# Attention with beacon keys, then an ELU MLP: a new order of the opening's loads and of all steps, tiles 0 and 1 with one ScalarE pass per ELU, and all copies of turned q and k of batches 1 and 2 on VectorE

## The chip, the cores and the metric

One core of one Trainium2 chip runs the kernel. The metric is the device time of one execution in microseconds (us), median of the runs; lower is better. Engines are named as in the profile: PE (TensorE matmul), PEld (its weight loads), DVE (VectorE), ACT (ScalarE), POOL (GpSimd), SP (SyncE). PSUM, which PE writes, has eight banks here, shared out by name: two "ops", two "hps", and two pairs "S".

## The reference

Inputs are float32: q, k, v of 8 batches x 8 heads x 576 tokens x 64, sixteen beacon keys and values for each batch and head, w_in 512 x 2048, w_out 2048 x 512. The attention is causal over the tokens, and the beacons are seen by all; then an MLP with ELU runs over 4608 tokens.

```python
scores = scale * np.matmul(q, k_all.transpose(0, 1, 3, 2))   # k_all: beacons first
scores = np.where(causal, -1000000000.0, scores)
a = np.exp(scores - scores.max(-1, keepdims=True))
a /= a.sum(-1, keepdims=True) + 1e-09
attn = np.matmul(a, v_all)
x = attn.transpose(0, 2, 1, 3).reshape(B * S, H * D)
h = x @ w_in
g = np.where(h > 0.0, h, np.exp(np.minimum(h, 0.0)) - 1.0)
return g @ w_out
```

## The kernel before

**An order written out by hand.** The kernel defines small steps (Python functions) and a text of 1489 words that says in which order they are issued, as "F.0.1" for F(0, 1). No scheduler changes that order: each engine runs its own instructions strictly in the order of the list, and waits where one needs something of another engine. So a step that waits holds up everything behind it on its engine, and DMAs issued by POOL wait behind POOL's other work. A DMA of POOL also waits, in both kernels, for the landing of the one eight issues ahead of it.

**Attention of a batch b** (p is a pair of heads, 0 to 3):

- lq (L132, issue L136) loads q and k through POOL, tokens on partitions; batch 0 in two runs of tokens (0 to 255, 256 to 575) and two halves of the heads, batch 1 in two halves of the heads, batch 2 whole. lv (L141, issues L144 and L149) loads v in five blocks of keys and the beacons' v. Batches 3 to 7 come instead through a scratch copy (lk, L754, POOL) and a transposing DMA (lt, L761, SP); lp (L769, L770, POOL) sets the beacon columns.
- T (L254, matmuls L266) turns q and k of a pair on PE, into an "hps" bank for batch 0 and an "S" pair for batches 1 and 2. ck (L283) copies the result out of PSUM on ACT, cq (L287) on DVE (both are recorded at L279). cb (L275) adds the beacon columns.
- S (L308, matmuls L320) makes scores by groups of columns into an "S" pair; x (L329, exp at L335) takes the exponential on ACT; m (L340) multiplies the causal mask on DVE (the mask is made on POOL by tri, L238 and L240).
- L (L401) makes the row sums, n (L434, L437) their inverse on ACT by a logarithm and an exponential, W (L377) the product with v, M (L471, L481, L488) scales it on DVE into xT, the input of the MLP. For batch 0 there are two parts of the tokens, A and B. D (L393, DVE) adds up exponentials ahead of L from batch 3 on.

**The MLP** runs over ten tiles of tokens: 0 and 1 of 256, the others of 512. F(t, i) (L502, matmuls L511) makes one bank "hps" of h from w_in, with sixteen F for a tile of 512 and eight for one of 256. The ELU has two forms:

```python
# u, k: two passes over PSUM on ACT (e and u), one instruction on DVE
e:  eb = exp(h)                     # ACT, L521
u:  rb = relu(h)                    # ACT, L526
kk: half = min(eb - 1, rb)          # DVE, L536, from SBUF
# r, g: one pass on ACT (e), two instructions on DVE
r:  rb = min(eb, 1) - 1             # DVE, L543, from SBUF
g:  half = max(h, rb)               # DVE, L548, reads h in PSUM
```

In the first form u frees the bank of h (e has read it too), in the second g does. G (L557) multiplies by w_out for tiles 0 and 1, o and s write them out. From tile 2 on the second product goes by a seven-product scheme of half tiles: Z (L578) forms sums of the activations on DVE, Q (L621) multiplies into "ops" banks, J (L630, L637, L635) moves and adds the results and stores them. wt (L578) forms the sums of w_out that it needs, and H (L578) those of w_in for the last tiles 8 and 9 (P, L691; K, E, U, V), where the first product uses seven products as well. The first H (H.1) writes into the tile that the beacon keys arrived in, which also holds the rows of zeros that the filler matmuls read.

**Loads of the weights.** wi(c) (L157, issues L161) loads half of w_in's columns in eight DMAs of 128 KB (as stored), wo (L164) a quarter of w_out in one of 512 KB. An F of tile 0 or 1 with i under 4 needs all eight DMAs of the first half.

**Fillers.** warm and wm (L205, L213) are matmuls into a bank that nobody reads, to keep PE busy; wm(n) has n units of 128 columns.

In the list of before, the loads stand between the steps: batch 0's q and k in four parts, v block 2, half of batch 1, v blocks 0 and 1, the first half of w_in, v blocks 3 and 4, the other half of batch 1, the second half of w_in, w_out.

Of the kernel before, what the change touches and what calls it, by code (L numbers as in the profile page):

```python
# [17 lines left out]
def kernel(  # L18
# [81 lines left out]
    w_in16 = konst.tile([P, NCC, DF], FP16, name="w_in16")  # L100
# [12 lines left out]
    st, vt = {}, {}  # L113
# [39 lines left out]

# [3 lines left out]
    def load_wi(c):  # L157
        f_ = slice(DF // 2 * c, DF // 2 * (c + 1))
        for g in range(2):
            for i in range(4):  # L160
                nc.gpsimd.dma_start(  # L161
                    out=w_in16[32 * i:32 * (i + 1), 2 * g:2 * g + 2, f_], in_=wi_v[i, :, g, :, f_])
# [86 lines left out]
    @step  # L249
    def wi(c):  # L250
        load_wi(c)
# [532 lines left out]
    lq.0.0.0.4 warm.12 ident bt T.0.1.0 bk cb.0.0 wm.7 T.0.0.0 ck.0.1.0 cb.0.1 S.0.1.0  # L784
    lq.0.1.0.4 cq.0.0.0 wm.8 T.0.0.1 cb.0.2 x.0.1.0 S.0.0.0 x.0.0.0 cq.0.0.1 T.0.1.1 wm.8
    S.0.0.2 tri lq.0.0.4.8 T.0.2.0 ck.0.1.1 S.0.1.2 T.0.3.0 x.0.0.2 cq.0.3.0 cq.0.2.0 x.0.1.2
    S.0.1.1 x.0.1.1 wm.6 S.0.1.3 cb.0.3 wm.6 S.0.3.0 x.0.1.3 lq.0.1.4.8 m.0.0.2 m.0.0.0 lv.0.2
    x.0.3.0 T.0.2.1 cq.0.2.1 S.0.0.3 x.0.0.3 wm.8 S.0.2.0 T.0.3.1 x.0.2.0 S.0.2.3 x.0.2.3
    m.0.3.0 cb.1.1 wm.4 S.0.2.2 cq.0.3.1 wm.6 S.0.3.3 lq.1.0.0.4 x.0.2.2 x.0.3.3 m.0.2.0 wm.6
    S.0.0.1 x.0.0.1 m.0.1.0 L.0.A T.1.0.0 lv.0.0.1 n.0.A cq.1.0.0 m.0.0.3 T.1.1.0 W.0.A.0  # L790
    W.0.A.1 M.0.A.0 M.0.A.1 m.0.1.3 S.0.2.1 cb.1.2 ck.1.1.0 m.0.2.2 cb.1.0 S.1.5 m.0.2.3 x.0.2.1
    wi.0 x.1.5 S.1.3 x.1.3 S.0.3.1 x.0.3.1 S.0.3.2 x.0.3.2 F.0.1 e.0.1 S.1.1 r.0.1 g.0.1 S.1.4
    x.1.4 F.0.0 S.1.2 F.0.2 x.1.1 x.1.2 u.0.0 lv.0.3.4 lq.1.0.4.8 e.0.2 m.0.3.2 m.0.1.2 m.0.3.3
    L.0.B n.0.B e.0.0 wi.1 W.0.B.0 M.0.B.0 W.0.B.1 M.0.B.1 wo.0 r.0.2 T.1.2.0 F.1.1 ck.1.2.0
    g.0.2 T.1.3.0 e.1.1 u.1.1 S.1.6 x.1.6 F.0.4 F.1.7 e.0.4 k.0.0 cq.1.3.0 S.1.11 S.1.7 m.1.1.0
# [137 lines left out]
```

## Time and profile before

| | us |
|---|---|
| median of three runs (335.95 to 339.8) | 336.29 |
| span of the profiled execution, first to last instruction | 335.3 |
| PE busy (share of the span) | 324.6 (97%) |
| PEld busy | 206.8 (62%) |
| DVE busy | 280.0 (84%) |
| ACT busy | 282.5 (84%) |
| POOL busy | 87.9 (26%) |

The span is that of one profiled execution; its whole time is not listed, and the median of the runs is 1.0 above the span. Idle time of an engine costs something only where the engine is on the chain that ends last. A busy PE is not PE at its peak: matmuls are pipelined and their ends are modelled, and the row counts a matmul as busy until its modelled end. In the page's view by slices the span is cut in 40 slices of 8.4 us; a digit is the busy share in tenths:

```profile
PE   7979899999999999999999999999999999999995
DVE  3652988666899999997999889988999998998962
ACT  2998798899999999989898889897987677988930
POOL 8875749360049106500160060000000000000000
DMA  9999999999939997996099495000101021010212
```

### The profile page before, as it was taken

The page shows a single profiled execution, that of the slowest core. Times are in us where ns is not written, and L with a number is a line of the kernel's source. Part 1 is how long each engine was busy: PE and PEld are TensorE (multiplying, and loading weights), DVE is VectorE, ACT ScalarE, POOL GpSimd, SP SyncE. Part 2 cuts the span into 40 slices and gives each one's busy share as a digit, 9 for nine tenths or more (in the row PEclk, how much of TensorE's full clock was granted, in tenths as well). Part 3 has the DMA queues.
Part 4 walks back from the last instruction along what each step waited for, and adds up shares of the span by engine and source line. Part 5 has one row for each costly group of instructions (what it writes and reads, how often), then busy time and mean ns, then how long its engine had stood idle before and what let it go on. Part 6 is the DMA issues. An engine that isn't in the chain of part 4 may idle for free.

```text
span 335.3 us, 8722 instructions
## 1 busy us (share of the span) xinstructions
PE 324.6 (97%) x3561; PEld 206.8 (62%) x3561; DVE 280.0 (84%) x592; ACT 282.5 (84%) x460; POOL 87.9 (26%) x121
## 2 busy tenths in 40 slices
PE   7979899999999999999999999999999999999995
PEld 3546666454446555657555656556555888688784
DVE  3652988666899999997999889988999998998962
ACT  2998798899999999989898889897987677988930
POOL 8875749360049106500160060000000000000000
PEclk9997999999999999999999999999999999999999
DMA  9999999999939997996099495000101021010212
GB/s 114 146 174 178 165 186 186 157 147 176 149 52 170 175 139 61 171 149 105 33 140 139 104 100 139 3 33 31 39 27 34 31 65 65 31 65 31 65 63 96
DMA packets 129080, 34.65 MB, mean 103 GB/s; under 512 B 112912, under 2 KB 127504, under 8 KB 129040
## 3 DMA queue, kind: packets, MB, share of 16 engines
q0 software_dynamic: 94912, 18.49, 68.6%
q1 hardware_dynamic: 33408, 15.34, 21.2%
q8 instruction: 28, 0.46, 0.6%
q10 hardware_dynamic: 720, 0.26, 0.3%
q14 instruction: 12, 0.10, 0.1%
HBM read 37.22 MB, written 15.34 MB: 157 GB/s over the span
## 4 chain that ended last, share of the span: by engine, by line
PE 53%; DVE 20%; ACT 11%; DMA 7%; POOL 4%; issue 3%; ACTq 0%; POOLq 0%
PE ops L621 20%; PE hps L511 16%; DVE gt L536 6%; PE hps L691 6%; DVE qk L393 5%; ACT et L335 4%; ACT e L521 3%; PE sc L320 3%; PE ops L557 3%; ACT r L526 3%; PE ut L377 3%; DMA v<-in_v_dram 2%; DMA kst<-in_k_dram 2%; DMA w_out<-in_moe_w_out_dram 2%; DVE et L340 2%
## 5 line engine op out<-in xcount | busy, mean ns | idle before, releaser
L511 PE MATMUL hps<-xT,w_in 128*128 128x512 f16 (+1 forms) x544 | 120.2, 357 | 0.7 <-DMA w_in<-in_moe_w_in_dram 0.5
L335 ACT ACTIVATE et<-sc 128x1024 f16<-128x1024 f32 (+2 forms) x114 | 104.7, 978 | 5.3 <-PE sc L320 5.3
L621 PEld LDWEIGHTS <-gt 128*128 128x128 f16 x768 | 74.1, 98 | 18.7 <-issue 1.7
L521 ACT ACTIVATE e<-hps 128x512 f32<-128x512 f32 x120 | 72.5, 622 | 7.7 <-PE hps L511 5.9
L511 PEld LDWEIGHTS <-w_in 128*128 128x128 f16 x544 | 49.8, 98 | 45.3 <-issue 7.9
L536 DVE SCALAR_TENSOR_TENSOR gt<-e,r 128x512 f16<-128x512 f32 x108 | 71.9, 682 | 6.7 <-ACT r L526 4.4
L526 ACT ACTIVATE r<-hps 128x512 f16<-128x512 f32 x108 | 65.3, 623 | 7.7 <-PE hps L511 4.4
L621 PE MATMUL ops<-wt,gt 128*128 128x256 f16 x384 | 50.1, 273 | 0.0
L621 PE MATMUL ops<-w_out,gt 128*128 128x256 f16 x384 | 49.6, 273 | 0.4 <-DVE osb L635 0.3
L149 POOL DMA_DIRECT2D v<-in_v_dram x40 | 36.0, 1048 | 5.5 <-DMA w_out<-in_moe_w_out_dram 2.4
L340 DVE TENSOR_TENSOR et<-et,triu 128x512 f16<-128x512 f16 (+4 forms) x108 | 31.6, 331 | 1.5 <-ACT et L335 1.5
L578 DVE TENSOR_TENSOR gt<-gt 128x1024 f16<-128x1024 f16 x48 | 32.4, 684 | 0.3
L393 DVE TENSOR_TENSOR qk<-qk,et 128x672 f16<-128x672 f16 (+2 forms) x60 | 21.8, 368 | 0.9
L377 PEld LDWEIGHTS <-v 128*32 128x32 f16 (+1 forms) x800 | 17.0, 96 | 8.7 <-issue 0.8
L377 PE MATMUL ut<-et,v 128*32 128x464 f16 (+3 forms) x560 | 21.0, 296 | 0.0
L637 DVE TENSOR_TENSOR osb<-ops,sm 128x512 f32<-128x512 f32 x24 | 16.4, 682 | 4.3 <-issue 3.3
L471 DVE TENSOR_TENSOR xT<-ut,rl 128x672 f16<-128x672 f32 (+12 forms) x26 | 16.4, 668 | 1.7 <-ACT rl L437 1.1
L621 PE MATMUL ops<-w_out,s 128*128 128x256 f16 x128 | 17.1, 273 | 0.0
L730 DVE SCALAR_TENSOR_TENSOR gt<-e,r 128x512 f16<-128x512 f32 x24 | 16.0, 685 | 0.8 <-ACT r L720 0.7
L144 POOL DMA_DIRECT2D v<-in_beacon_v_dram x8 | 6.5, 812 | 38.4 <-PE ut L377 38.4
L557 PE MATMUL ops<-w_out,gt 128*128 128x512 f16 x64 | 16.0, 380 | 0.6 <-DMA w_out<-in_moe_w_out_dram 0.6
L621 PEld LDWEIGHTS <-s 128*128 128x128 f16 x128 | 12.4, 98 | 3.0
(108 smaller groups left out, 394.8 us busy)
## 6 DMA issues: line engine op xcount, KB each, us to landing
out_dram<-osb SPq DMA_DIRECT2D x35, 256.0 KB, 2.3
v<-in_v_dram POOLq DMA_DIRECT2D x24, 128.0 KB, 7.1
scr<-in_q_dram POOLq DMA_DIRECT2D x5, 576.0 KB, 13.8
scr<-in_k_dram POOLq DMA_DIRECT2D x5, 576.0 KB, 15.4
w_in<-in_moe_w_in_dram POOLq DMA_DIRECT2D x16, 128.0 KB, 7.5
w_out<-in_moe_w_out_dram POOLq DMA_DIRECT2D x4, 512.0 KB, 9.4
v<-in_v_dram POOLq DMA_DIRECT2D x8, 112.0 KB, 9.7
v<-in_v_dram POOLq DMA_DIRECT2D x8, 80.0 KB, 6.7
```

Source lines behind the costliest of these rows:

```text
L149: nc.gpsimd.dma_start(out=vt[b][r0:r0 + n, j, :, :], in_=v[b, :, ilo[j]:ilo[j] + n, :].rearrange("h s d -> s h d"),)
L335: nc.scalar.activation(out=ets[b, d][:, :, a - EC2 * d:e - EC2 * d], in_=sc[b, g][:, :, a - c0:e - c0], func=AFT.Exp, bias=0.0, scale=SCALE)
L340: nc.vector.tensor_tensor(out=o, in0=o, in1=i, op=ALU.mult)
L377: nc.tensor.matmul(out=t[32 * i:32 * (i + 1), a - qa:e - qa], lhsT=ones[0:kc[j], :] if half is None else v16[0:kc[j], j, h, 32 * half:32 * ...
L393: (nc.vector if eng == "v" else nc.gpsimd).tensor_tensor(out=o, in0=t[0:rows, :, a:e] if n == 0 else o, in1=t[0:rows, :, col:col + e - a], ...
L511: nc.tensor.matmul(out=h[:, n_, :], lhsT=w_in16[:, cc, P * fc:P * (fc + 1)], rhs=xt[k][:, cc, a - TT * k:e - TT * k], start=(cc == 0), sto ...
L521: nc.scalar.activation(out=eb[t, i], in_=flat(hp[t, i]), func=AFT.Exp, bias=0.0, scale=1.0)
L526: nc.scalar.activation(out=rb[t, i], in_=flat(hp[t, i]), func=AFT.Relu, bias=0.0, scale=1.0)
L536: nc.vector.scalar_tensor_tensor(out=half(t, i), in0=eb[t, i], scalar=1.0, in1=rb[t, i], op0=ALU.subtract, op1=ALU.min)
L557: nc.tensor.matmul(out=ob[t, tb_], lhsT=gt[:, fc, P * tb_:P * (tb_ + 1)], rhs=w_out16[:, fc, :], start=(fc == 0), stop=(fc == NFC - 1))
L578: (nc.vector if eng == "v" else nc.gpsimd).tensor_tensor(out=o_, in0=a_, in1=b_, op=op_)
L621: nc.tensor.matmul(out=xy[t, n_][:, qd, :], lhsT=lw[:, P * qd:P * (qd + 1)], rhs=wt_[:, c, :], start=(first and qd == 0 and c == 0), stop= ...
```

## The change

- **Loads.** wi now issues one DMA per step and lv one block per step; the beacons' v is issued behind block 0 rather than ahead of all. The number of DMAs is the same. In the list all of batch 0's q and k come first, then three of the eight DMAs of w_in's first half, v blocks 1, 2, 0, the five others, half of batch 1, v blocks 4 and 3, the other half of batch 1, then w_in's second half with a first quarter of w_out in it. The identity matrix (ident) is made behind four of the loads, the mask (tri) behind eleven.
- **ELU of tiles 0 and 1.** All sixteen F use e, r, g. Before, nine did and seven used e, u, k; u and k go from 108 each to 101, r and g from 12 each to 19.
- **Copies.** The four ck of batches 1 and 2 (ck.1.1.0, ck.1.2.0, ck.2.2.0, ck.2.3.0) are cq now. The two ck of batch 0 stay.
- **Fillers.** wm goes from 59 units in nine steps to 42 in ten, and some now stand behind L.0.A and behind H.1.1.
- **Order.** The list is new throughout. In the opening, exponentials of batch 1 come behind the first four F. H.1.0 and H.1.1 stand right behind M.0.A.1 (before: H.1.1 near the first F of tile 2, H.1.0 far later), and ahead of L.3.0 stand eight of the twelve H (before: two) and all eight wt (before: six). lk.5.1 stands ahead of lk.3.0.

The diff, with the two lists cut behind their first 24 lines (in the changed kernel the issues of v and of the beacons' v are L147 and L152; the lines of the other steps are the same):

```diff
@@ -141,8 +141,6 @@
     def load_v(b, js):
         if b not in vt:
             vt[b] = stage.tile([P, NKC, H, D], FP16, tag="v16", name="v16")
-            nc.gpsimd.dma_start(
-                out=vt[b][0:NB, 0, :, :], in_=beacon_v[b].rearrange("h n d -> n h d"))
         for j in js:
             r0 = NB if j == 0 else 0
             n = kc[j] - r0
@@ -150,16 +148,18 @@
                 out=vt[b][r0:r0 + n, j, :, :],
                 in_=v[b, :, ilo[j]:ilo[j] + n, :].rearrange("h s d -> s h d"),
             )
+            if j == 0:
+                nc.gpsimd.dma_start(
+                    out=vt[b][0:NB, 0, :, :], in_=beacon_v[b].rearrange("h n d -> n h d"))
 
     wi_v = moe_w_in.rearrange("(g i t d) f -> i d g t f", i=4, t=2, d=32)
     wo_v = moe_w_out.rearrange("(f p) m -> p f m", p=P)
 
-    def load_wi(c):
+    def load_wi(c, n):
         f_ = slice(DF // 2 * c, DF // 2 * (c + 1))
-        for g in range(2):
-            for i in range(4):
-                nc.gpsimd.dma_start(
-                    out=w_in16[32 * i:32 * (i + 1), 2 * g:2 * g + 2, f_], in_=wi_v[i, :, g, :, f_])
+        g, i = n // 4, n % 4
+        nc.gpsimd.dma_start(
+            out=w_in16[32 * i:32 * (i + 1), 2 * g:2 * g + 2, f_], in_=wi_v[i, :, g, :, f_])
 
     def load_wo(i):
         nc.gpsimd.dma_start(out=w_out16[:, 4 * i:4 * (i + 1), :], in_=wo_v[:, 4 * i:4 * (i + 1), :])
@@ -247,8 +247,8 @@
         load_qk(b, n_, h0, h1)
 
     @step
-    def wi(c):
-        load_wi(c)
+    def wi(c, n):
+        load_wi(c, n)
 
     @step
     def T(b, p, n_):
     run("""
-    lq.0.0.0.4 warm.12 ident bt T.0.1.0 bk cb.0.0 wm.7 T.0.0.0 ck.0.1.0 cb.0.1 S.0.1.0
-    lq.0.1.0.4 cq.0.0.0 wm.8 T.0.0.1 cb.0.2 x.0.1.0 S.0.0.0 x.0.0.0 cq.0.0.1 T.0.1.1 wm.8
-    S.0.0.2 tri lq.0.0.4.8 T.0.2.0 ck.0.1.1 S.0.1.2 T.0.3.0 x.0.0.2 cq.0.3.0 cq.0.2.0 x.0.1.2
-    S.0.1.1 x.0.1.1 wm.6 S.0.1.3 cb.0.3 wm.6 S.0.3.0 x.0.1.3 lq.0.1.4.8 m.0.0.2 m.0.0.0 lv.0.2
-    x.0.3.0 T.0.2.1 cq.0.2.1 S.0.0.3 x.0.0.3 wm.8 S.0.2.0 T.0.3.1 x.0.2.0 S.0.2.3 x.0.2.3
-    m.0.3.0 cb.1.1 wm.4 S.0.2.2 cq.0.3.1 wm.6 S.0.3.3 lq.1.0.0.4 x.0.2.2 x.0.3.3 m.0.2.0 wm.6
-    S.0.0.1 x.0.0.1 m.0.1.0 L.0.A T.1.0.0 lv.0.0.1 n.0.A cq.1.0.0 m.0.0.3 T.1.1.0 W.0.A.0
-    W.0.A.1 M.0.A.0 M.0.A.1 m.0.1.3 S.0.2.1 cb.1.2 ck.1.1.0 m.0.2.2 cb.1.0 S.1.5 m.0.2.3 x.0.2.1
-    wi.0 x.1.5 S.1.3 x.1.3 S.0.3.1 x.0.3.1 S.0.3.2 x.0.3.2 F.0.1 e.0.1 S.1.1 r.0.1 g.0.1 S.1.4
-    x.1.4 F.0.0 S.1.2 F.0.2 x.1.1 x.1.2 u.0.0 lv.0.3.4 lq.1.0.4.8 e.0.2 m.0.3.2 m.0.1.2 m.0.3.3
-    L.0.B n.0.B e.0.0 wi.1 W.0.B.0 M.0.B.0 W.0.B.1 M.0.B.1 wo.0 r.0.2 T.1.2.0 F.1.1 ck.1.2.0
-    g.0.2 T.1.3.0 e.1.1 u.1.1 S.1.6 x.1.6 F.0.4 F.1.7 e.0.4 k.0.0 cq.1.3.0 S.1.11 S.1.7 m.1.1.0
-    cb.1.3 r.0.4 g.0.4 e.1.7 r.1.7 lq.2.0.0.8 G.0.0.0 x.1.7 F.0.5 x.1.11 e.0.5 S.1.12 g.1.7
-    cb.2.1 m.1.2.0 x.1.12 S.1.0 F.0.7 r.0.5 G.0.1.0 S.1.8 x.1.0 g.0.5 F.1.5 e.0.7 x.1.8 m.1.3.1
-    S.1.10 cb.2.0 m.1.1.1 S.1.9 e.1.5 x.1.10 r.0.7 g.0.7 cb.2.2 lv.1.0.1 wo.1 r.1.5 g.1.5 x.1.9
-    F.1.0 u.1.0 e.1.0 m.1.0.0 T.2.0.0 cq.2.0.0 F.0.3 T.2.1.0 cq.2.1.0 T.2.2.0 e.0.3 u.0.3
-    m.1.2.1 k.0.3 wt.1.0 k.1.1 ck.2.2.0 F.1.4 F.0.6 e.0.6 S.2.0 S.2.5 x.2.5 x.2.0 r.0.6 m.1.3.0
-    G.0.0.1 m.1.0.1 g.0.6 G.0.1.1 k.1.0 lv.1.2.3.4 lp.3.0 lp.3.1 T.2.3.0 e.1.4 ck.2.3.0 L.1.1
-    n.1.1 F.1.2 r.1.4 u.1.2 e.1.2 M.1.1.0 W.1.1 M.1.1.1 S.2.3 F.1.3 x.2.3 L.1.0 W.1.0 n.1.0 wo.2
-    M.1.0.0 M.1.0.1 u.1.3 e.1.3 wo.3 g.1.4 G.0.0.2 S.2.1 x.2.1 F.2.13 wt.1.1 e.2.13 S.2.4 lk.3.0
-    lk.3.1 lt.3.0 x.2.4 S.2.8 x.2.8 k.1.2 cb.2.3 G.0.1.2 F.2.0 u.2.0 u.2.13 S.2.7 x.2.7 k.1.3
-    S.2.9 x.2.9 e.2.0 G.0.0.3 o.0.0 G.0.1.3 F.2.3 e.2.3 S.2.10 m.2.0.0 S.2.2 r.2.3 g.2.3 k.2.0
-    x.2.10 x.2.2 G.1.0.0 F.2.11 e.2.11 u.2.11 S.2.6 S.2.12 lv.2.2.3.4 x.2.6 F.2.1 u.2.1 e.2.1
-    m.2.1.0 F.1.6 G.1.0.1 m.2.2.1 x.2.12 k.2.13 F.2.7 e.2.7 m.2.0.1 m.2.1.1 k.2.11 u.2.7 k.2.7
...
+    lq.0.0.0.4 lq.0.1.0.4 ident lq.0.0.4.8 lq.0.1.4.8 wi.0.5 wi.0.4 wi.0.7 tri lv.0.1 lv.0.2 lv.0.0
+    wi.0.1 wi.0.0 wi.0.2 wi.0.3 wi.0.6 lq.1.0.4.8 lv.0.4 lv.0.3 lq.1.0.0.4 wi.1.6 wo.0 wi.1.1 wi.1.7
+    wi.1.4 wi.1.5 wi.1.0 wi.1.3 wi.1.2 wo.1 warm.12 bt bk T.0.0.0 wm.4 T.0.1.0 ck.0.1.0 cb.0.0
+    cb.0.3 cb.0.1 cq.0.0.0 wm.4 S.0.0.0 S.0.1.0 x.0.1.0 T.0.0.1 x.0.0.0 cq.0.0.1 m.0.1.0 m.0.0.0
+    T.0.1.1 wm.4 S.0.0.1 ck.0.1.1 wm.4 S.0.1.2 T.0.3.0 x.0.0.1 x.0.1.2 cb.0.2 T.0.2.0 S.0.0.3
+    cq.0.3.0 x.0.0.3 cq.0.2.0 m.0.1.2 S.0.3.0 wm.3 S.0.2.0 x.0.3.0 m.0.3.0 T.0.2.1 S.0.1.1 m.0.0.3
+    x.0.2.0 T.0.3.1 cq.0.2.1 lq.2.0.0.8 x.0.1.1 lv.1.0 m.0.2.0 cq.0.3.1 cb.1.0 wo.2 wo.3 lv.1.4
+    S.0.1.3 lv.1.3 S.0.0.2 lv.1.2 x.0.1.3 x.0.0.2 m.0.0.2 lv.1.1 lk.5.1 m.0.1.3 wm.3 S.0.2.3 L.0.A
+    lk.3.0 cb.1.1 S.0.2.1 cb.1.2 x.0.2.3 m.0.2.3 wm.7 W.0.A.0 n.0.A M.0.A.0 S.0.3.1 W.0.A.1 cb.1.3
+    x.0.3.1 M.0.A.1 x.0.2.1 H.1.0 H.1.1 wm.4 S.0.2.2 x.0.2.2 m.0.2.2 wm.3 S.0.3.3 F.0.2 e.0.2 r.0.2
+    F.0.1 e.0.1 g.0.2 x.0.3.3 S.0.3.2 r.0.1 g.0.1 x.0.3.2 m.0.3.3 wm.6 F.0.3 e.0.3 r.0.3 F.0.0 e.0.0
+    m.0.3.2 r.0.0 g.0.3 L.0.B g.0.0 n.0.B W.0.B.0 M.0.B.0 W.0.B.1 lv.2.0 lk.3.1 lk.4.0 lv.2.2
+    M.0.B.1 lv.2.3 T.1.3.0 lv.2.1 cq.1.3.0 F.1.3 lv.2.4 e.1.3 F.1.1 S.1.11 r.1.3 e.1.1 S.1.12 x.1.11
+    x.1.12 g.1.3 r.1.1 g.1.1 F.1.0 e.1.0 T.1.1.0 T.1.0.0 cq.1.1.0 cq.1.0.0 r.1.0 g.1.0 m.1.3.1
+    G.0.1.0 S.1.4 F.1.2 S.1.3 x.1.4 e.1.2 x.1.3 cb.2.1 S.1.1 x.1.1 r.1.2 g.1.2 H.1.2 G.0.0.0 m.1.1.0
+    S.1.2 x.1.2 F.0.6 e.0.6 r.0.6 g.0.6 F.1.4 e.1.4 r.1.4 g.1.4 S.1.5 T.1.2.0 x.1.5 cq.1.2.0 lt.3.0
+    lp.3.0 F.0.7 e.0.7 lt.3.1 S.1.0 r.0.7 x.1.0 g.0.7 lk.7.0 cb.2.0 wt.1.0 m.1.0.1 lk.4.1 F.0.4
+    e.0.4 wt.2.0 lp.3.1 G.0.1.1 S.1.7 r.0.4 g.0.4 S.1.8 x.1.7 x.1.8 F.0.5 m.1.0.0 e.0.5 r.0.5
+    G.0.0.1 S.1.6 S.1.9 x.1.6 x.1.9 m.1.1.1 cb.2.2 g.0.5 F.1.5 T.2.0.0 cq.2.0.0 e.1.5 T.2.1.0
+    cq.2.1.0 wt.4.0 m.1.2.1 m.1.2.0 r.1.5 F.1.6 e.1.6 L.1.0 n.1.0 M.1.0.0 S.2.5 g.1.5 r.1.6 wt.1.1
+    x.2.5 wt.2.1 G.0.0.2 G.0.1.2 S.2.1 g.1.6 x.2.1 S.2.0 x.2.0 m.2.0.0 G.0.1.3 G.0.0.3 o.0.1 o.0.0
+    s.0.1 S.1.10 S.2.4 s.0.0 x.1.10 cb.2.3 x.2.4 m.1.3.0 F.1.7 e.1.7 T.2.3.0 cq.2.3.0 r.1.7 wt.4.1
+    W.1.0 L.1.1 M.1.0.1 g.1.7 n.1.1 M.1.1.0 G.1.0.0 G.1.1.0 S.2.10 x.2.10 W.1.1 lv.3.1 lv.3.3
+    M.1.1.1 T.2.2.0 F.2.13 lv.3.2 u.2.13 F.2.3 e.2.13 lv.3.0 cq.2.2.0 e.2.3 r.2.3 g.2.3 S.2.12
...
```

## The prediction

> **What bounds the kernel now.** I read the table by stage first (the stages cut at the breaks of the chain), then the chain of waits, the timeline where TensorE begins on w_in, and the rows by form for prices. Columns of the first fence: stage, its length, busy time of PE, PEld, DVE, ACT, POOL (instructions), granted clock, DMA share, GB/s.
>
> ```profile
> 8.00:18.00 10.00, 9.90 (x163) 5.05 (x157) 6.64 (x22) 9.45 (x13) 7.65 (x13) 1.00 1.42 146
> 18.00:25.40 7.40, 4.92 (x150) 3.34 (x146) 3.95 (x12) 6.97 (x10) 5.80 (x11) 1.00 1.35 178
> 25.40:28.80 3.40, 3.10 (x18) 1.65 (x19) 0.89 (x2) 1.81 (x3) 2.09 (x4) 0.51 1.36 176
> 28.80:40.30 11.50, 10.47 (x227) 7.67 (x226) 7.30 (x17) 9.87 (x16) 7.26 (x10) 1.00 1.11 170
> 40.30:84.70 44.40, 44.33 (x570) 24.87 (x569) 32.34 (x71) 40.34 (x61) 22.18 (x22) 1.00 1.99 173
> 84.70:115.00 30.30, 30.30 (x318) 15.59 (x318) 26.81 (x56) 30.24 (x49) 12.87 (x15) 1.00 1.50 129
> 115.00:254.00 139.00, 138.05 (x1404) 83.49 (x1403) 130.65 (x282) 125.73 (x207) 23.31 (x33) 1.00 0.78 88
> ```
>
> From 40.3 us on PE is never idle by its row; before that it waits, and at 25.4 to 28.8 us it runs at 0.51 of its clock. ACT is full at 84.7 to 115 us (30.24 of 30.30), DVE nearly full behind that (130.65 of 139). DVE has room early: 12 of 44.4 us are free at 40.3 to 84.7.
>
> ```profile
> 23.64 7.99 DMA kst<-in_k_dram
> ...
> 32.43 7.80 DMA w_out<-in_moe_w_out_dram
> 40.23 0.04 issue
> 40.27 1.02 PE ops L557 x4
> 41.29 0.87 PE hps L511 x8
> ...
> 82.20 1.86 PE hps L511 x8
> 84.06 0.02 issue
> 84.09 0.60 ACT e L521
> ```
>
> The chain is loads up to 40.23, then 44 us of PE without a gap, then ACT; behind 115 us it changes between DVE and PE. So what is lost is lost in the first 40 us, and a step is worth what PE has done when it becomes gapless.
>
> ```profile
> 25.70 1.44 PE L511 MATMUL hps<-xT,w_in 128*128 128x256 f16 x6 [0.52 <-DMA w_in<-in_moe_w_in_dram]
> 27.18 0.60 ACT L521 ACTIVATE e<-hps 128x512 f32<-128x512 f32 x1 [1.22 <-PE hps L511]
> 27.81 0.43 DVE L543 TENSOR_SCALAR r<-e 128x512 f16<-128x512 f32 x1 [4.27 <-ACT e L521]
> ```
>
> The first half of w_in is in at about 25.6 us; that starts the MLP, ACT waits 1.22 us for it and DVE 4.27.
>
> ```profile
> L526 ACT ACTIVATE r<-hps 128x512 f16<-128x512 f32 x108 | 65.3, 623 | 7.7 <-PE hps L511 4.4 <-DVE gt L536 2.5 <-DVE qk L393 0.5
> L536 DVE SCALAR_TENSOR_TENSOR gt<-e,r 128x512 f16<-128x512 f32 x108 | 71.9, 682 | 6.7 <-ACT r L526 4.4 <-ACT e L521 2.1
> L548 DVE TENSOR_TENSOR gt<-hps,r 128x512 f16<-128x512 f32 x12 | 8.3, 688 | 0.7
> L543 DVE TENSOR_SCALAR r<-e 128x512 f16<-128x512 f32 x12 | 6.3, 525 | 7.4 <-ACT e L521 7.3
> L279 DVE COPY qk<-tp 128x1152 bf16<-128x1152 bf16 x3 | 4.1, 1357 | 2.5 <-PE tp L266 2.4
> L279 ACT COPY hi<-tp 128x1152 bf16<-128x1152 bf16 x3 | 3.4, 1119 | 1.4 <-PE tp L266 1.3
> ```
>
> **The change, part by part.**
>
> *ELU and copies.* Seven of tiles 0 and 1 go from u and k to r and g. ACT loses 7 x 0.60 (65.3/108) = 4.2 us; DVE loses 7 x 0.67 and gains 7 x (0.53 + 0.69): +3.8. Four copies move: ACT -4 x 1.12 = -4.5, DVE +4 x 1.36 = +5.4. Together ACT -8.7, DVE +9.2, all before about 77 us. Two buffers are held longer: that of F is freed by g, behind e and r, instead of by u; that of T by a copy in DVE's queue.
>
> *Loads.* In front of the first F the old order has 3136 KB (batch 0 q and k 1152, all the v of blocks 0 to 2 384, half of batch 1 576, half of w_in 1024), the new one 2560. The 576 KB, at the 146 to 178 GB/s of the stages, are 3.3 to 4.0 us: w_in's first half at 21.6 to 22.3 instead of 25.6. Bounds: 20 (the triangle mask's 1.1 us on POOL is now behind three w_in issues too) and 25.6 (w_in pieces no faster). I take 21.8. POOL's issues are as many as before, and each waits for the landing of the one eight before it in both orders. Half of batch 1, the second half of w_in and the first w_out chunk follow by about 36 to 39; in the old order they came at 31.6 to 40.2. The scratch copy of batch 5's k now stands ahead of batch 3's: 576 KB, 3.3 us at 173 GB/s. On SP, stores s.0.* stand behind both transposes of batch 3; batch 3's first S comes behind 85 us and these land at some 80, so it is covered by some 5 us; if not, ACT's stage at 85 us begins that much later.
>
> *A new wait.* H.1.0 and H.1.1 now stand on DVE right behind M.0.A.1. They need the first half of w_in, and write rows that the filler matmuls read. So wm.4 on PE waits for H.1.1, and behind it S.0.2.2 and x.0.2.2; on DVE the mask and r.0.2. H costs 4 x 0.28 = 1.1: S.0.2.2 starts at 21.8 + 1.1 = 22.9, about 2 us after ACT runs dry. Fillers fall from 59 to 42 units; PE waits there, so I cost them at nothing but for the clock, below.
>
> *The opening, laid out.* Behind 22.9: S.0.2.2 and S.0.3.3 (0.33 each: x8 took 0.54 in the chain, and a step has 528/107 = 4.9 matmuls), F.0.2 at 23.6. Two buffers of F then turn over in F 0.98 + e 0.60 + r 0.53 + g 0.69 = 2.8, so a pair of F per 2.8 us: the fourth F ends at 28.4 to 28.9. L.0.B 1.25, n.0.B 1.35, M.0.B 1.7: M.0.B.1 ends at 33 (34.29 + 0.88 = 35.2 before). A half-clock stretch like that of 25.4 adds up to 1.7 (half of 3.4), so 33 to 34.7. Up to G.0.0.0, DVE then has 3 copies x 1.36 + 4 x (0.53 + 0.69) + masks 0.6 + H 0.6 = 10.2, of which the last 1.8 lie behind what G waits for: G.0.0.0 at 41.4 to 43.1; 42.0 with a part of the cold stretch.
>
> Before, G.0.0.0 started at 40.27, with F 6 done, G 0, S 24, T 4 of batch 1. In the new list it has F 8, G 1, S 21, T 3 ahead of it. PE is further by 2 x 0.98 + 0.86 - 3 x 0.33 - 0.63 = 1.2 (the chain's times for F, G, S and T). Break-even is 41.5, so the opening loses 0.5 (from -1.5, with w_in at 20, to +3).
>
> *G.0.0.0 to L.1.0.* DVE has 14.6 us listed there (copies 3, r and g 5 pairs, masks, wt) and 1.8 left over, PE 14.4 (F 7, G 2, S 7, T 3, L and H of batch 1). Before, PE had no gap. Between 0 and +2: +1.0, nearer to full loss since DVE's queue has two long copies at its end.
>
> *84.7 to 115.* Adding up each engine's rows of this trace along both lists up to L.3.0 (an instruction counted until the next one starts): ACT 98.1 before, 91.4 after; DVE 76.9 and 94.1; F 39 and 40, Q 5 and 8. From L.2.0 to L.3.0 ACT has 29.7 instead of 31.3: -1.6 at most, 0 if PE ends it. I take -1.0.
>
> *115 to 254.* Behind L.3.0 DVE has 193.6 left instead of 202.0, since six more H, two wt and three Z are done by then: -8.4. The chain is on DVE for half of this stage (so -4.2 at most), yet PE's row is idle for 0.95 of 139 only. I take -1.5, nearer to PE's row.
>
> Sum: 0.5 + 1.0 - 1.0 - 1.5 = -1.0 on the profiled execution's span of 335.3: 334.3. Its time with what lies around the span is not listed; the median of the three runs, 336.29, is 1.0 above the span, so 335.3.
>
> *The clock.* PE has 4.92 busy of 7.40 us just ahead of the 0.51 stretch, and six 256-wide matmuls took 1.44, against eight in 0.98 in the chain. I count a part of one such stretch in the new kernel's opening, as laid out. The Trainium skill ("TensorE: Matmul & The Clock Gate", Part 1: The HAM clock gate) says that an idle window of about 3.4 us halves the clock and a busy one restores it. By that rule the pause at 19 to 23 us would bring a whole halved window and the sum would be 337.0; the trace's one stretch, behind a sparse 7 us, agrees with it.
>
> **The rivals.**
>
> *Relief of ACT pays (faster).* Up to L.3.0 ACT works 98.1 us of the 106 since its first copy at 7.1, 92%. If ACT, not PE, sets that whole part, its 6.7 us less are worth 6.7/0.92 = 7.3: 329.0. For it: ACT is full at 84.7 to 115. Against: the chain has no ACT between 40 and 84.
>
> *DVE takes over (slower).* From G.0.0.0 to L.3.0 DVE has 66.3 + 1.8 = 68.1 us. L.3.0 would come at 116.6 at equal standing (113.4 before, and one F and three Q more, 3.2). At the 88% that DVE reached at 84.7 to 115 it needs 77 us: 42 + 77 = 119, +2.8. At its 73% of 40.3 to 84.7 it needs 93: +19. It costs over 6.7 from a share under 84% on (68.1/81.3). For it: g and the copies now hold PSUM buffers in one queue. Price at 82%: 345.
>
> *The load order changes nothing.* If w_in lands at 25.6 as before, G.0.0.0 moves by 3.8: 339.1. Against: 576 KB fewer ahead.
>
> *A whole cold stretch more.* DVE's new wait leaves PE almost without work from the end of W.0.A, about 19 us, to 23. If that is enough for a stretch like the one at 25.4, and the F behind it wait for it in full, +1.7: 337.0. For it: the clock fell behind 7.4 us with 4.92 busy. Against: fillers (wm.7) stand at the start of the pause. It is the rule of the page named above.
>
> **How the numbers follow.** No measurable change 0.52 (335.3; own range 331 to 339.5); a cold stretch more 0.10 (337.0); loads unmoved 0.08 (339.1); relief of ACT 0.16 (329.0); DVE takes over 0.14 (345). 2% of the median is 6.7, about what a measurement tells from no change: 329.6 and 343.0. Faster 0.16, within 0.70, slower 0.14. The range for 8 in 10 takes in most of the ACT case and the milder DVE cases: 329 to 342.
>
> **What would show it.** The first F (L511) starting at 23 to 25 instead of 24.8, the first G (L557) at 38 to 42; DVE busy over 85% of 40 to 85 us (73% before) and ACT under 85% (91%); S (L320) waiting for DVE copies instead of ACT; DVE less full behind 115. It is wrong if PE has gaps of over 3 us in sum behind 42 us, if w_in is in at 25 or later, or if PE's end-to-end gapless part begins before 38 us.

## The result: 348.3 us, 3.4% slower, and the profile after

The changed kernel takes 348.34 us (median of four runs, 346.9 to 351.35) against 336.32 for the kernel before; the ratio is 1.034, its 95% interval 1.026 to 1.042. The profiled execution took 348.25 with a span of 346.5, 11.2 more than before. Times and ratios below leave out executions that a slower state of the chip disturbed.

The table by stage with the same cuts as before (stage, length, busy time of PE, PEld, DVE, ACT, POOL, granted clock, DMA share, GB/s), changed kernel:

```profile
8.00:18.00 10.00, 8.08 (x168) 5.21 (x167) 7.35 (x27) 9.47 (x13) 8.56 (x16) 0.90 1.53 161
18.00:25.40 7.40, 4.29 (x83) 2.22 (x74) 3.16 (x13) 3.95 (x6) 5.61 (x9) 0.73 1.39 178
25.40:28.80 3.40, 2.78 (x21) 1.77 (x20) 1.03 (x2) 1.90 (x4) 1.89 (x4) 0.88 1.29 203
28.80:40.30 11.50, 10.29 (x233) 8.16 (x233) 9.13 (x20) 6.87 (x11) 7.65 (x11) 1.00 1.14 183
40.30:84.70 44.40, 39.87 (x528) 22.89 (x524) 40.60 (x72) 30.68 (x44) 26.51 (x25) 1.00 1.94 161
84.70:115.00 30.30, 29.88 (x333) 15.29 (x328) 25.96 (x60) 29.65 (x49) 9.12 (x9) 1.00 1.19 109
115.00:254.00 139.00, 135.22 (x1393) 81.65 (x1391) 124.24 (x261) 127.10 (x207) 29.70 (x36) 1.00 0.81 93
```

The cuts stand at the same times as before, not at the same work. PE's busy column locates the loss: 4.5 us less at 40.3 to 84.7 (39.87 against 44.33), 0.4 at 84.7 to 115, 2.8 at 115 to 254 (135.22 against 138.05). That is 7.7. Behind 254 PE is idle for 5.0 us (87.50 busy of 92.50) against 4.0 before (77.30 of 81.30), nearly all of it behind its last matmul, and the 2.5 that are left of the 11.2 belong to the time before 40.3, where the clock is under 1.00 in three stages instead of one. ACT is down to 30.68 of 44.4 in the middle stage, DVE up from 32.34 to 40.60.

The chain of waits of the changed kernel (start, length, what):

```profile
34.94 10.46 DMA kst<-in_k_dram
...
49.56 1.27 DVE hi L279
50.83 2.42 DVE r L543
53.34 0.69 DVE gt L548
...
57.25 1.16 DVE r L543
59.57 2.39 DVE qk L279 x2
...
121.82 7.03 DMA kst<-scr
```

Before, the chain was PE without a gap from 40 to 84 us. Now it is loads to 45, then DVE to 74, and at 121.82 a transposing DMA. (DVE's own rows show no wait at 45.4, where the chain passes from the load to DVE, so how much the loads up to there cost is not shown.) Over the whole run PE waits for transposing DMAs in two places (total, times, longest); before, it never did:

```profile
PE sc L320 <- DMA kst<-scr: 3.1, 2, 1.8
```

Most of the loss is seen in an instruction and what PE waits for. First the opening, PE's and then DVE's row by time:

```profile
20.88 0.56 PE L377 MATMUL ua<-et,v 128*32 128x256 f16 x24 [0.61 <-DVE xT L481]
23.60 0.53 PE L320 MATMUL sc<-hi 64*128 64x224 bf16 x4 [2.16 <-DVE lo L578]
24.06 0.50 PE L213 MATMUL w<-lo 128*128 128x384 bf16 x1
24.50 0.53 PE L320 MATMUL sc<-hi 64*128 64x128 bf16 x6
24.96 2.51 PE L511 MATMUL hps<-xT,w_in 128*128 128x256 f16 x16
```

```profile
21.51 0.69 DVE L481 TENSOR_TENSOR xT<-ua,rl 128x512 f16<-128x512 f32 x1 [0.61 <-PE ua L377]
22.12 0.89 DVE L578 TENSOR_TENSOR lo<-w_in 128x256 f16<-128x256 f16 x4
```

The first half of w_in had landed at 21.05 us, but the first F starts only at 24.96: PE waits 2.16 us for H.1.1 (lo, L578). H itself stands in DVE's queue behind M.0.A.1 (L481) and starts without a wait for w_in. The 16 matmuls of the first two F then take 2.51 us, in part at half clock (16 took 2.05 before, at 37.09). Second, DVE and POOL at 50 us:

```profile
49.48 1.35 DVE L279 COPY hi<-tp 128x1152 bf16<-128x1152 bf16 x1
50.74 2.49 DVE L543 TENSOR_SCALAR r<-e 128x512 f16<-128x512 f32 x1
53.34 0.69 DVE L548 TENSOR_TENSOR gt<-hps,r 128x512 f16<-128x512 f32 x1
```

```profile
48.53 2.23 POOL L754 DMA_DIRECT2D scr<-in_k_dram  x1
50.23 2.75 POOL L754 DMA_DIRECT2D scr<-in_q_dram  x1
```

```profile
54.08 1.03 PE L511 MATMUL hps<-xT,w_in 128*128 128x256 f16 x8 [2.03 <-DVE gt L548]
```

An r (L543) of 0.42 us is on DVE for 2.49, to 53.23: 0.25 behind the end of POOL's second issue of a scratch copy (50.23 + 2.75 = 52.98). The g behind it frees the bank that F waits for, 2.03 us. By groups, x and mean ns:

```profile
L543 DVE TENSOR_SCALAR r<-e 128x512 f16<-128x512 f32 x19 | 12.6, 662 | 4.4 <-ACT e L521 4.4
```

A mean of 662 ns hides that eleven of the nineteen took 0.41 to 0.43 us and five 0.73 to 2.49. In the kernel before it was 525, by the same cause (one took 1.04 us beside scratch copies at 53.4).

### The profile page after: what moved, and what is told of

Its sections match the earlier page's. It is cut to its first block, busy times and chain, and to the rows that moved or that the text cites. A ratio compares the mean times of both kernels' runs of the same rounds, so it can differ in the third digit from the quotient of the medians.

```text
span 346.5 us, 8724 instructions
## 1 busy us (share of the span) xinstructions
PE 324.3 (94%) x3553; PEld 208.3 (60%) x3556; DVE 293.1 (85%) x603; ACT 275.2 (79%) x449; POOL 95.8 (28%) x121
## 4 chain that ended last, share of the span: by engine, by line
PE 57%; DVE 15%; DMA 11%; ACT 7%; POOL 4%; issue 4%; SPq 0%; DVEq 0%; POOLq 0%
PE ops L621 24%; PE hps L511 19%; PE sc L320 5%; PE hps L691 4%; DMA kst<-scr 4%; PE ut L377 3%; DMA w_out<-in_moe_w_out_dram 3%; DMA kst<-in_k_dram 3%; DVE r L543 2%; ACT et L335 2%; ACT e L521 2%; ACT r L526 2%; DMA v<-in_v_dram 2%; DVE gt L548 2%; DVE et L340 2%
## 5 line engine op out<-in xcount | busy, mean ns | idle before, releaser
L511 PE MATMUL hps<-xT,w_in 128*128 128x512 f16 (+1 forms) x544 | 118.7, 356 | 4.8 <-DVE gt L548 4.6
L521 ACT ACTIVATE e<-hps 128x512 f32<-128x512 f32 x120 | 74.0, 626 | 14.9 <-PE hps L511 13.4
L511 PEld LDWEIGHTS <-w_in 128*128 128x128 f16 x544 | 50.6, 98 | 47.4 <-issue 10.7
L536 DVE SCALAR_TENSOR_TENSOR gt<-e,r 128x512 f16<-128x512 f32 x101 | 67.7, 683 | 9.1 <-ACT e L521 6.1
L526 ACT ACTIVATE r<-hps 128x512 f16<-128x512 f32 x101 | 62.2, 635 | 9.2 <-PE hps L511 9.1
L147 POOL DMA_DIRECT2D v<-in_v_dram x40 | 37.3, 1060 | 58.5 <-PE ut L377 30.0
L578 DVE TENSOR_TENSOR gt<-gt 128x1024 f16<-128x1024 f16 x48 | 32.3, 683 | 0.4
L377 PEld LDWEIGHTS <-v 128*32 128x32 f16 (+1 forms) x800 | 17.7, 96 | 11.0 <-issue 3.6
L730 DVE SCALAR_TENSOR_TENSOR gt<-e,r 128x512 f16<-128x512 f32 x24 | 16.1, 684 | 0.3 <-ACT r L720 0.2
L543 DVE TENSOR_SCALAR r<-e 128x512 f16<-128x512 f32 x19 | 12.6, 662 | 4.4 <-ACT e L521 4.4
L320 PE MATMUL sc<-kst 64*128 64x208 bf16 (+13 forms) x160 | 12.1, 252 | 3.3 <-DMA kst<-scr 3.1
```

What stands on the lines that cost most here:

```text
L147: nc.gpsimd.dma_start(out=vt[b][r0:r0 + n, j, :, :], in_=v[b, :, ilo[j]:ilo[j] + n, :].rearrange("h s d -> s h d"),)
L320: nc.tensor.matmul(out=s[:, h, a - c0:e - c0], lhsT=t[D * h:D * (h + 1), 1, P * j:P * (j + 1)], rhs=t[D * h:D * (h + 1), 0, NB + qa + a - ...
L377: nc.tensor.matmul(out=t[32 * i:32 * (i + 1), a - qa:e - qa], lhsT=ones[0:kc[j], :] if half is None else v16[0:kc[j], j, h, 32 * half:32 * ...
L511: nc.tensor.matmul(out=h[:, n_, :], lhsT=w_in16[:, cc, P * fc:P * (fc + 1)], rhs=xt[k][:, cc, a - TT * k:e - TT * k], start=(cc == 0), sto ...
L521: nc.scalar.activation(out=eb[t, i], in_=flat(hp[t, i]), func=AFT.Exp, bias=0.0, scale=1.0)
L526: nc.scalar.activation(out=rb[t, i], in_=flat(hp[t, i]), func=AFT.Relu, bias=0.0, scale=1.0)
```

## The experiments

The theories (D was formed after a_ck and a_h, E after a_hukl): A, DVE's load itself; B, the new wait for H.1.1 in the opening; C, the order of the list as a whole; D, r stretched while POOL issues scratch copies; E, the transposing DMAs being late because scratch copies run beside them.

**The change's own parts undone, one by one.**

a_uk: the seven ELU pieces back (and u, k likewise for the other six)

```diff
- r.0.0 ... g.0.0   (also 0.3 1.0 1.1 1.2 1.3 1.6)
+ u.0.0 ... k.0.0
```

> The changed kernel with the seven ELU pieces that the change moved (0.0, 0.3, 1.0, 1.1, 1.2, 1.3, 1.6) back in the old form, in the same places of the list: relu on ScalarE (u), one pass on VectorE (k). VectorE loses 7 x (0.43 + 0.69 - 0.68) = 3 us, ScalarE gains 7 x 0.62 = 4.3 us. Theory A (VectorE's load at 45 to 70 us, where it is 9.9 of 10 busy, makes some 4 of the 12 us lost): 345 to 346, since only one of the seven lies behind 45 us. Theory B (the order of the opening and its new wait make the loss): 347.5 to 349. Theory C (the list as a whole, no single edit): 348.

345.9 and 350.1 us, ratio 1.033 [1.025, 1.041]: no clear gain (changed kernel 1.034). An r of 2.27 us at 50.56 is still there.

a_ck: the four copies back

```diff
- cq.1.1.0 cq.1.2.0 cq.2.2.0 cq.2.3.0
+ ck.1.1.0 ck.1.2.0 ck.2.2.0 ck.2.3.0
```

> The changed kernel with the four copies of turned q and k that the change gave to VectorE back on ScalarE (1.1.0, 1.2.0, 2.2.0, 2.3.0), in the same places. VectorE loses 4 x 1.36 = 5.4 us, ScalarE gains 4 x 1.12 = 4.5 us. Theory A (VectorE's load): two of the four lie at 40 to 70 us where VectorE ends the steps, 2.7 us there: 345.5 to 347. Theory B and C: 348 to 349, as ScalarE is not idle enough at 85 to 115 us for the last two.

Ratio 1.038 [1.034, 1.042]: no gain either. POOL issues the scratch copies 2.5 us earlier than in the changed kernel (at 46.02 for 48.53), and an r that starts at 47.14 meets two of them: 3.58 us, with a 6.8 us half-clock stretch behind it. Theory A's forecast lies below this interval; a_uk's interval is too wide to shut it out.

a_h: the new wait taken away

```diff
- M.0.A.1 x.0.2.1 H.1.0 H.1.1 wm.4 S.0.2.2
+ M.0.A.1 x.0.2.1 wm.4 S.0.2.2
- g.1.2 H.1.2
+ g.1.2 H.1.0 H.1.1 H.1.2
```

> The changed kernel with H.1.0 and H.1.1 (the sums of w_in's rows, which wait for its first half and hold the fillers, a score step, its exponential and the first F behind them) moved from ahead of the fillers at 21 us to H.1.2 at 42 us. Theory B (this wait and the pause of TensorE at 20 to 30 us that follows, with a second half-clock stretch, cost 3 to 5 us): 344 to 346, TensorE's wait of 2.16 us at 23.6 and one half-clock stretch gone. Theory A: 348 or up to 349, since the opening is given back by 45 us while VectorE has 1.1 us more to do at 42. Theory C: 348.

344.4 and 346.8 us, the second one profiled. The first F starts at 21.35 instead of 24.96, and in this execution there is no half-clock stretch before 50 us:

```profile
21.35 1.81 PE L511 MATMUL hps<-xT,w_in 128*128 128x256 f16 x15
```

Then the gain is eaten (DVE, and PE, of a_h):

```profile
48.97 3.53 DVE L543 TENSOR_SCALAR r<-e 128x512 f16<-128x512 f32 x1
```

```profile
53.35 1.87 PE L511 MATMUL hps<-xT,w_in 128*128 128x256 f16 x8 [3.39 <-DVE gt L548]
55.14 0.69 PE L266 MATMUL tp<-identb,qst 96*64 96x96 bf16 x12
```

POOL's issues of the two scratch copies end at 52.24, r at 52.50. PE pauses 3.39 us and then runs at half clock for 6.8 us (T takes 0.69, else 0.45). The execution of 344.4 us had a mean clock of 0.997, which leaves no room for such a stretch. So B is right for the opening, and D decides what of it arrives.

a_ukl: seven other ELU pieces back, those whose r lay at 48 to 71 us

```diff
- r.0.7 ... g.0.7   (also 1.4 0.4 0.5 1.5 1.6 1.7)
+ u.0.7 ... k.0.7
```

> The changed kernel with seven other ELU pieces in the old form, those whose first VectorE pass (L543) lay at 48 to 71 us and took 0.73, 2.49, 0.42, 1.24, 0.41, 0.63 and 0.93 us, 6.9 together: 1.4, 0.7, 0.4, 0.5, 1.5, 1.6, 1.7. VectorE loses about 6.9 us just where it is full, ScalarE gains 4.3 us where it is 6.3 to 7.2 of 10 busy. Theory A (VectorE full, its long L543 instructions above all, costs 4 us at 45 to 70): 343.5 to 345, and the stretched 2.49 us one is gone while the one-pass form beside the same POOL issues stays at 0.68. Theory B (opening) and C: 347 to 349.

342.7 and 345.4 us, ratio 1.021 [1.015, 1.027]. With as many pieces undone as in a_uk, 4 us are gained (the intervals just overlap): the place counts more than the number. A had forecast this; since the stretched r at 50 us is gone too, D explains it as well, and this run doesn't tell the two apart.

a_ord: H moved, the change's seven pieces and four copies undone together, only order and loads left

> The order of the changed list and its load order alone: H.1.0 and H.1.1 at H.1.2, the seven ELU pieces of the change back in the old form, the four copies back on ScalarE. VectorE loses 9.2 us, ScalarE gains 8.7. Theory B plus A (new wait and VectorE's load): 338 to 341. Theory D (nine L543 instructions are left, and those at 47 to 60 us still meet the scratch copies): 344 to 347. Theory C (the order itself): 347 to 350.

345.3, ratio 1.025 [1.017, 1.033], as D had it: no better than moving H alone. So with the seven pieces and the four copies undone, the new order and loads still cost some 8.5 us. An r of 1.98 us is left at 51.03 and one of 2.23 at 75.78.

a_hukl: the edits of a_h and a_ukl

> The changed kernel with H.1.0 and H.1.1 at H.1.2 and the seven ELU pieces 1.4, 0.7, 0.4, 0.5, 1.5, 1.6, 1.7 in the old one-pass form: both of the single edits that moved PE's work ahead. With H moved alone, PE was 4.6 us ahead of the changed kernel up to 48 us, and lost it in one 3.53 us L543 instruction beside the scratch copies and a 6.8 us half-clock stretch behind it; the other edit alone left PE 5 us ahead. Theory B plus D (the two add up): 338 to 341. If at 50 to 60 us something else sets the pace at a fixed time (a load, a buffer): 342 to 344, as with the one edit.

340.4, ratio 1.010 [1.003, 1.018]: they add up (2.8 and 4.3 us by the single edits, 7.9 together). No r is over 0.43 us. This kernel has as many two-pass ELUs as a_ord and four copies more on DVE, and is 5 us faster.

**Stretching or load?** a_rp: r with a second source

```diff
- nc.vector.tensor_scalar(
-     out=rb[t, i], in0=eb[t, i], scalar1=1.0, scalar2=1.0, op0=ALU.min, op1=ALU.subtract)
+ nc.vector.scalar_tensor_tensor(
+     out=rb[t, i], in0=eb[t, i], scalar=1.0, in1=ones[:, 0:1].broadcast_to([P, 512]),
+     op0=ALU.min, op1=ALU.subtract)
```

> The changed kernel with the first VectorE pass of the two-pass ELU (L543, one source, 0.42 us, but 0.6 to 2.5 us and in other runs 3.6 us when it meets a scratch copy that POOL is issuing; it then ends 0.25 us after the POOL instruction) written as a two-source instruction, min(e, 1) - ones. k, which has two sources, took 0.68 us beside the same POOL issues, so all 16 should now take about 0.68: VectorE has 16 x 0.26 = 4.2 us more of its own work and 4.6 us of stretching less. Theory D (the stretching itself costs 2 to 4 us at 47 to 60): no L543 instruction over 0.8 us, and 344 to 347 although VectorE has as much to do. Theory A (VectorE's load, whatever it is made of): 348 to 351. If the stretching is no matter of the second source, 2 us ones are still there.

346.15, ratio 1.027 [1.021, 1.033]. The group of r, and the r beside the two scratch copies (issued 46.82 to 51.27), in a_rp:

```profile
L543 DVE SCALAR_TENSOR_TENSOR r<-e,ones 128x512 f16<-128x512 f32 x19 | 13.0, 685 | 3.6 <-ACT e L521 3.4
```

```profile
50.63 0.68 DVE L543 SCALAR_TENSOR_TENSOR r<-e,ones 128x512 f16<-128x512 f32 x1
```

Each r takes 0.68 to 0.69, also beside POOL. DVE's total for r is 13.0 instead of 12.6, and still 2.2 us are gained. The intervals overlap, but all four runs (345.84 to 346.87) lie below the changed kernel's fastest (346.9), and A's forecast lies just outside the interval: it is the length of single instructions on the chain that costs, not DVE's sum. c_hrp adds a_h's edit:

> The changed kernel with H.1.0 and H.1.1 at H.1.2 and the first ELU pass with two sources; ELU and copies stay as the change has them. H alone gave 344 to 347 us, the two sources alone 346.1. Theory B plus D: PE keeps the 4.6 us that moving H gives at 45 us, since no 3.5 us instruction stands at 49: 341 to 343. Theory A (VectorE is full at 45 to 70 with 4 us more to do, and takes them back): 345 to 347.

343.2, ratio 1.019 [1.014, 1.023]: moving H is worth 2.9 here, the sum just above what B and D said and below what A said.

**One part alone, in the kernel before.** b_e has the seven ELU pieces, b_c the four copies, b_ec both.

```diff
- e.0.0 ... u.0.0 ... k.0.0   (also 0.3 1.0 1.1 1.2 1.3 1.6)
+ e.0.0 ... r.0.0 g.0.0
- ck.1.1.0 ck.1.2.0 ck.2.2.0 ck.2.3.0
+ cq.1.1.0 cq.1.2.0 cq.2.2.0 cq.2.3.0
```

> The kernel before with the seven ELU pieces of the change in two VectorE passes and nothing else (with the four copies too it took 350.6, 13.8 us more than before). Theory A (VectorE's load): +3.8 us of VectorE's work where 12 of 44 us are free: 337 to 341. Theory D (L543 instructions that meet a scratch copy of POOL): one of 2.8 us or so at 48 to 52: 340 to 343. If the two parts add up evenly by their VectorE time (3.8 and 5.4 of 9.2): 342.5.

> The kernel before with the four copies of turned q and k on VectorE and nothing else. VectorE +5.4 us, ScalarE -4.5. Theory A: the copies hold PE's turned batches behind a queue of masks, g and k: 339 to 345, with the loss at the places of the first two copies, 32 to 48 us. If the two parts add up evenly by VectorE time: 345. If ScalarE's relief pays: 333 to 335.

> The kernel before, in its own order and with its own loads, with the change's seven ELU pieces in two VectorE passes (placed right behind their exponentials) and the four copies on VectorE. Theory A (VectorE's load alone makes the change slow): 340 to 343. Theory D: between, 337 to 341, by how many L543 instructions meet scratch copies at 49 to 84 us. Theory C and B (order and opening): 335.5 to 337. If relief of ScalarE pays: 333 to 335.

348.1 (1.031 [1.026, 1.036]), 346.8 (1.026 [1.021, 1.032]) and 350.6 (1.039 [1.034, 1.044]): each part alone costs about as much as the whole change, and together little more. None of the forecasts reached these numbers. All three have an r of 2.8 to 3.7 us at 48 to 50 us and a half-clock stretch behind it. So I took the stretching of r away in two of them, by the two-source r:

> The kernel before with the change's four copies on VectorE (346.8 us) and the first ELU pass with two sources. VectorE has 12 x 0.26 = 3 us more. Theory D (the 3.68 us instruction at 47.94 and the half-clock stretch behind it make 5 of the 9 us): 341 to 343, what is left being the cold 6.8 us at 22.9. Theory A: 347 to 350.

> The kernel before with the change's seven ELU pieces and four copies (350.6 us), and the first ELU pass written with two sources, so that it takes 0.68 us whatever POOL issues. VectorE has 4 to 5 us more of its own work. Theory D (the meeting with the scratch copies makes most of the 13.8 us): 342 to 345. Theory A (VectorE's load itself): 351 to 355.

c_bcrp takes 344.0 (1.019 [1.014, 1.023]), 2.8 less; c_becrp 353.2 (1.045 [1.039, 1.050]), no less than b_ec. Here D fails as the main cause: in the old order DVE's queue itself is what PE waits for. In c_bcrp (and in b_c, by the same 2.8) the S of the opening waits for a copy of turned q and k that ACT made before, and 6.8 us at half clock begin in that pause, at 23.0; later another S waits 2.29 us for another of the four copies. The first wait in c_bcrp (total, times, longest), then the second on PE and on DVE:

```profile
PE sc L320 <- DVE qk L279: 2.8, 1, 2.8
```

```profile
57.10 0.61 PE L320 MATMUL sc<-qk 64*128 64x144 bf16 x6 [2.29 <-DVE hi L279]
```

```profile
53.89 0.68 DVE L536 SCALAR_TENSOR_TENSOR gt<-e,r 128x512 f16<-128x512 f32 x1
54.49 0.68 DVE L579 TENSOR_TENSOR wt<-w_out 128x1024 f16<-128x1024 f16 x1
55.09 0.68 DVE L536 SCALAR_TENSOR_TENSOR gt<-e,r 128x512 f16<-128x512 f32 x1
55.70 1.35 DVE L279 COPY hi<-tp 128x1152 bf16<-128x1152 bf16 x1
```

The copy that the later S needs stands behind two k and a wt; 2.29 us of pause, and PE runs at half clock for 3.4 us from 57.1. The price of stretching in the old order stays open between nothing and 2.8.

**The transposing DMAs.** In a_hukl 2.5 us are left here (PE):

```profile
123.44 0.28 PE L320 MATMUL sc<-kst 64*128 64x256 bf16 x2 [2.50 <-DMA kst<-scr]
```

a_huklk moves two scratch copies behind lt.4.1, c_best moves them ahead:

```diff
# a_huklk
+ lp.5.0 lk.6.1 lk.6.0
# c_best
+ lv.3.4 lk.5.0 lk.6.1 ... lv.4.0 lk.6.0
```

> The kernel with H moved and seven ELU pieces in the one-pass form (340.4 us), and the scratch copies of batch 6 (lk.6.1, lk.6.0), which POOL issued at 114.1 and 146.4 us beside the transposing transfers of batch 4 and 5, moved behind lp.5.0, some 15 us later for the first. Theory E (the copy of 576 KB running from 114.1 to 124.6 makes the second transposing transfer, 115.29 to 123.30, take 8.0 us where undisturbed ones took 3.7 to 4.4; PE waits 2.7 us for it): it lands at 119 to 120, PE's gap behind it is gone, 337 to 338. If the transfer is late for its own issue or its buffer: 340 to 341.

346.9, ratio 1.027 [1.021, 1.033]. The wait at 123 is gone as E had it: lt.4.1's second transfer took 3.7 us (115.45 to 119.18) instead of 8.0. But the copies now ran at 126 to 145, with v's loads behind them, and the next four transfers took 8.5 to 10.3 us; PE waited 4.8 and 1.7 us for them. These waits are 3.0 us more than a_hukl's 3.5; the kernel is 6.5 slower, and where the rest goes was not traced.

> The kernel with H moved and seven ELU pieces in one pass (340.4 us), with the scratch copies lk.5.0 and lk.6.1 ahead of batch 4's v on POOL, so that they run at 85 to 110 us where POOL issued nothing, and lk.6.0 at 108 instead of 146. Theory E: the transposing transfers of batch 4 and 5 (113 to 119, 129 to 134, 143 to 149) meet no scratch copy, PE's gap of 2.7 us at 120 to 125 is gone and nothing is given back later as when the copies were put at 126 to 145: 336.5 to 338, level with the kernel before. If the transfers are late for another reason, or the early copies hold batch 4's own transposing transfers at 100 to 106: 340 or more.

340.2 to 344.5 us, ratio 1.014 [1.007, 1.021], no better than a_hukl. The wait at 123 is gone here too, but lt.4.0's transfers at 101 to 108 now meet a copy. So E's mechanism is shown (in these three runs, behind 100 us, a transfer with no copy beside it took 3.5 to 4.7 us, beside a copy or the loads queued behind it 4.8 to 10.3), a gain from it is not. The kernel before has late transfers too (10.6 and 9.3 us at 138 to 151, beside two scratch copies), and its PE waits for none of them: in its order the S that needs a transfer comes after it has landed.

**A mixture.** d_mix: a_rp and a_h, and four pieces (1.4, 0.7, 0.4, 0.5) back

> The changed kernel with H.1.0 and H.1.1 at H.1.2, the first ELU pass with two sources, and four ELU pieces (1.4, 0.7, 0.4, 0.5) in the one-pass form; the other twelve of batch 0 stay in two passes of 0.68 and 0.69 us. Between c_hrp (343.2, none of them back) and the kernel with seven back (340.4). If ScalarE sets the pace at 40 to 90 us in the latter, three pieces less (1.9 us) make it 337.5 to 339. If VectorE's load still counts there: 341 to 343. If what is left is the order of the list: 340 to 341.

341.5, ratio 1.013 [1.007, 1.019], what was forecast if DVE's load still counts there. No version beat the kernel before.

## Why the prediction was wrong

- **The opening, "loses 0.5 (from -1.5 to +3)": inside its range, 1.5 worse than the point.** The first half of w_in landed at 21.05 for 21.8 and S.0.2.2 started at 23.60 for 22.9, but G.0.0.0 (the second G of this list; the first, G.0.1.0, is at 40.61) started at 43.48 for 42.0. The break-even of 41.5 holds: by the matmul records 16 of S are missing ahead of G.0.0.0 (104 against 120), at 0.07 each 1.1 us where I took three S at 0.33. So the opening lost 2.0, near the 2.5 that the table leaves for it.
- **The new wait, laid out but not weighed.** The prediction put H.1.1 into the opening (S.0.2.2 at 22.9) and never asked what the opening would do without it. Moving H shows that: G.0.0.0 starts at 38.88 in a_h for 43.48, and at 40.09 in c_hrp for 43.14 in a_rp, and 2.8 to 3.7 us are gained in three pairs (changed kernel and a_h, a_rp and c_hrp, a_ukl and a_hukl).
- **"G.0.0.0 to L.1.0: +1.0": the step that failed.** From G.0.0.0 (43.48) to L.1.0 (60.89) PE was busy for 13.71 of 17.41 us, so it lost 3.7, and 4.5 up to 84.7. I priced r by the row's mean, 0.53, as if that were its work. It is 0.42 and a wait for POOL, so it costs 0.42 or 2.49 by what POOL issues at that moment: three r in this stretch took 0.73, 2.49 and 1.24, which is 3.2 us of waiting. The scratch copies I had counted only by their bytes. The rival "DVE takes over" (345, chance 0.14) had the place right and the size nearly; its mechanism, a DVE share under 84%, was not what came. DVE was 91% busy (40.60 of 44.4), a part of that being the wait inside r.
- **"84.7 to 115: -1.0" and "115 to 254: -1.5": failed.** They were +0.4 and +2.8, and 1.0 came behind 254, where I had put nothing (it lies in the last copies and stores behind PE's end, and no run explains it). ACT stayed full at 85 to 115 (29.65 of 30.30), and its relief earlier bought nothing since PE stood behind DVE. Behind 115 DVE had more room, as said (124.24 for 130.65), but PE waited 3.1 us for transposing DMAs, which I had looked at for batch 3 only.
- **The clock.** The profiled execution had the whole half-clock stretch more of the rival (granted clock 0.90 and 0.73 at 8 to 25.4; stretches at 16.0 to 19.4 and 22.8 to 26.2). It is not what makes the kernel slow: another execution of it had a mean clock of 0.995, as the kernel before with its one stretch, and took 348.42. The rule of the Trainium skill named in the prediction agrees with the length: 3.41 us per stretch in the trace. It does not agree in what comes ahead of one: in the 3.4 us ahead of these two stretches PE was not idle but busy for 2.58 and 1.43 us.
- **"It is wrong if PE has gaps of over 3 us in sum behind 42 us"**: this was the sign, 4.5 us in the middle stage alone.

What the parts are worth in the changed kernel: the wait for H some 3 to 4 of the 12 us (so that the earlier load gave nothing), two-pass ELUs at 48 to 71 us some 4 to 5 (2.2 of it comes back when r no longer stretches), and 3.5 are left in a_hukl. Its trace shows 3.5 of waits for transposing DMAs (2.5 and 1.0), but c_best, with 1.2 of such waits, is no faster, so what the 3.5 are made of stays open. That the rest is the order of the list is argued, not shown.

## What to carry to other kernels

A row's mean is a price only if its instructions have one length: look at the longest, and at what another engine does beside them. In a list order without slack, shifting work by 1 or 2 us changes which instructions meet, so a change "where there is room" is priced at the instant, in the queue, and not by the share of busy time. A wait that seems free because PE is idle still counts everything behind it on its queue, and the cold clock after it.

## What the runs showed of the hardware

- **DVE waits for POOL's DMA issuing.** r, one source and a result in SBUF, took 0.42 us alone and up to 3.68 us (b_c) beside POOL's issues of scratch copies (2.2 to 2.75 us each). It mostly ended 0.25 us behind the end of such an issue (53.23 and 52.98, 58.41 and 58.17 in the changed kernel, 52.50 and 52.24 in a_h, 50.72 and 50.47 in a_ck), in some cases 0.6 (51.62 and 50.99 in b_c). An r that started only 0.2 us into an issue was not held: 0.42 at 48.17 in a_uk, with the issue from 47.97 to 50.36. With a second source in SBUF r took 0.68 beside the same issues. The Trainium skill ("SBUF — State Buffer", Who interferes with whom) says that DVE and GpSimd share a port pair as a lock, held for a whole instruction by whichever comes first, and that one-source instructions in a two-port mode take it while two-source ones meet GpSimd only where it reads SBUF. These runs agree, except that POOL does not hold DVE from the first moment of its record. The warning of the Trainium skill (SBUF: two separate sides) is of DVE holding up the writing of descriptors; here it went the other way.
- **Copies and transposing transfers slow each other**: behind 100 us, 3.5 to 4.7 us for a transfer alone, 4.8 to 10.3 beside a copy or the loads queued behind it (a_hukl, a_huklk, c_best); a copy of 576 KB took 8.2 to 10.5 us in a_hukl behind 107 us, and 15 to 17 in a_huklk beside four transfers and v.
- **One long pause of PE costs more than itself**: 3.39 us of wait in a_h were followed by 6.8 us at half clock. The number of such stretches differs between executions of one kernel: the profiled one of the changed kernel had two, and another, with a mean clock of 0.995, room for one at most.
